# Building a small identity tile by DMA instead of by a GpSimd select, a first GpSimd maximum on zeros, and a buffer of its own for each of the last four results

## The chip, the cores and the metric

The kernel runs on one core of a Trainium2 chip. The metric is the device time of one execution in microseconds, as the median of several runs; lower is better. The engines are TensorE (PE, with its weight loads shown apart as PEld), VectorE (DVE), ScalarE (ACT), GpSimd (POOL) and the queue that issues the transfers (SP).

## The reference, cut to what matters

Linear attention with a learned feature map, then two MLPs without a residual. Shapes: batch 4, 8 heads, 576 positions, head dimension 64, 128 features, model width 512, hidden width 2048.

```python
def phi(x):
    proj = np.einsum('bhsd,df->bhsf', x, w_phi)
    proj = proj - np.max(np.abs(proj), axis=-1, keepdims=True)
    return np.concatenate([np.exp(proj), np.exp(-proj)], axis=-1)
q_p, k_p = phi(q), phi(k)
kv = np.einsum('bhsf,bhsd->bhfd', k_p, v)
z = np.sum(k_p, axis=2)
num = np.einsum('bhsf,bhfd->bhsd', q_p, kv)
den = np.einsum('bhsf,bhf->bhs', q_p, z)[..., None] + 1e-06
attn = num / den                        # then reshaped to 2304 tokens x 512
h = attn @ w_in;  x = (h * sigmoid(h)) @ w_out
h = np.maximum(x @ w_in2, 0.0);  out = (h * h) @ w_out2
```

The weights arrive as 64-bit floats (the kernel sees pairs of 32-bit words and converts them on DVE).

## The kernel before

Tokens are cut into 8 blocks of 288 columns. Each MLP handles a block in 16 chunks of 128 hidden units; the attention of the next blocks (keys of batch j and head pair p, queries of half batch b and head pair p) is mixed in between the chunks of the blocks before it. Most operands are split into a rounded high part and a low rest, so most products are three matmuls; keys and queries of the first blocks are multiplied whole.

No order of work is written out by hand. Every step is handed to a planner as an operation with an engine, a cost in ns, a key, and what it reads and writes (`op(key, engine, cost, emit, r=, w=, bufs=)`). The planner plays the engines through in its own time: on each idle engine the ready operation with the lowest key starts, if its buffers are free. A transfer costs it 640 ns on the queue, then its size at 240 bytes per ns behind all transfers before it, then 1500 ns (L70). ACT and DVE operations that belong to no unit get their key lowered by 202.77 (L86). The instructions are issued in the order that this gives, on five in-order queues; on the chip each waits for its own inputs. All transfers go through SP.

The start of the kernel, which the change touches:

- `phi_load` (L354) brings the feature weights into `wbl`, over zeros that `blank` set on DVE.
- `phi_zero` (L362) runs first on POOL, at a cost of 9000 in the plan: it builds the 65x65 identity `ident` with `make_identity` (a memset, masks.py:197, and an affine select, masks.py:199) and sets `wbl_hi` and `wbl_lo` to zero.
- `phi_hi` (L371, ACT) and `phi_lo` (L377, DVE) then split the feature weights into the high and low tiles that later blocks use.
- `queries_of` projects queries on PE (L792), copies them out on ACT (L798), takes the largest magnitude over all 128 partitions on POOL (`peak`, L805, tile `qm`), subtracts it on DVE (L811, tile `qp`) and exponentiates on ACT (L823, tile `qe`).
- `keys_of` projects keys (L602), takes their maximum (L607) and subtracts it (L613) on DVE, exponentiates (L690, tile `kp`), sets a column of ones in the value tile `v` on POOL (`ones`, L548) and multiplies features and values (L706, tile `pkv`). `v` has two buffers.
- The identity is read only by the transposes of `turn` (L732), from batch 2 on.

The end: the last chunk of a block copies its four accumulators to tiles `y` (L990 on ACT for d = 0 and 2, L992 on DVE for d = 1 and 3) and stores each (L995). These tiles have the tag `o`, with two buffers. The tag `xx`, also two buffers of the same shape, holds the attention's results `x`.

```python
LAT = {"PE": 450, "SP": 150}
DMA_ISSUE, DMA_LAT, DMA_RATE = 640, 1500, 240.0
...
op(T0 - 99, "POOL", 9000, phi_zero, w=["wbl0", "ident"])
op(P["phi"], "ACT", 1200, phi_hi, r=["wraw", "wbl0"], w=["phi_hi"])
op(P["phi"], "DVE", 1200, phi_lo, r=["wraw", "phi_hi"], w=["phi_lo"])
```

Of the kernel before, what the change touches and what calls it, by code (L numbers as in the profile page):

```python
# [9 lines left out]

F32 = mybir.dt.float32
F32R = mybir.dt.float32r
# [9 lines left out]
HB = S // 2  # L22
NB = NTOK // HB
# [5 lines left out]
D1 = D + 1  # L29
# [36 lines left out]
class Plan:  # L66
# [15 lines left out]
    def op(self, key, engine, cost, emit, r=(), w=(), bufs=(), unit=None, after=()):  # L82
        if unit and engine == "PE":
            key -= KEYS["pe"]
        if not unit and engine in ("ACT", "DVE"):
            key -= KEYS["el"]  # L86
        o = Op(len(self.ops), key, engine, cost, emit, unit)
        before = set(after)
        for x in r:
            before.update(self.written[x])  # L90
        for x in w:
            before.update(self.read.pop(x, ()))
            before.update(self.written.get(x, ()))
        for x in r:
            self.read.setdefault(x, []).append(o)
        for x in w:
            self.written[x] = [o]
        if unit and unit.token:
            bufs = [*bufs, unit.token]
        for b in bufs:  # L100
            if b not in self.started:
                self.started.add(b)
                b.first = o
                o.allocs.append(b)
                if b.pool in self.last:
                    self.last[b.pool][0] += 1
            else:
                before.add(b.first)
            b.users += 1
            o.frees.append(b)  # L110
        before.discard(o)
        o.waits = len(before)
        for x in before:
            x.after.append(o)
        self.ops.append(o)
        if unit:
            unit.ops.append(o)
        return o
# [131 lines left out]
def act(n, psum=False):  # L250
    return (51 if psum else 93) + 0.833 * n + 60


def dve(n, fast=False):
    return 70 + (0.52 if fast else 1.04) * n + 60
# [6 lines left out]
def dma(kb):  # L262
    return kb
# [14 lines left out]
def attention_then_two_mlps(ctx, tc, kT, qT, v, w_phi, w1, w2, out):  # L278
    nc = tc.nc
    P = KEYS  # L280
# [12 lines left out]
    sp = ctx.enter_context(tc.tile_pool(name="sp", bufs=2))  # L293
# [24 lines left out]
    op = plan.op  # L318
# [6 lines left out]
    def bank(name, unit, pool_="att"):  # L325
        if pool_ == "att" and unit.early == 2:
            pool_ = "eb"
        return Buf(pool_, lambda: psb.tile([128, 512], F32, tag="b", name=name), unit)

    def get(b):  # L330
        if b.tile is None:
            b.tile = b.make()
        return b.tile


    def hi_act(dst, src):
        nc.scalar.copy(out=dst, in_=src)  # L337

    def lo_on(engine, dst, src, hi):
        e = nc.vector if engine == "DVE" else nc.gpsimd  # L340
        e.tensor_tensor(out=dst, in0=src, in1=hi.bitcast(F32), op=ALU.subtract)  # L341
# [8 lines left out]
    ident = const.tile([D1, D1], F32, name="ident")  # L350
# [8 lines left out]
    def blank():  # L359
        nc.vector.memset(wbl, 0.0)  # L360

    def phi_zero():  # L362
        make_identity(nc, ident)
        nc.gpsimd.memset(wbl_hi.bitcast(F32), 0.0)
        nc.gpsimd.memset(wbl_lo.bitcast(F32), 0.0)

# [16 lines left out]
    T0 = -60.0  # L383
    op(T0 - 99, "DVE", 200, blank, w=["blank"])
    op(T0 - 99, "SP", dma(64), phi_load, r=["blank"], w=["wraw"])
    op(T0 - 99, "POOL", 9000, phi_zero, w=["wbl0", "ident"])
    op(P["phi"], "ACT", 1200, phi_hi, r=["wraw", "wbl0"], w=["phi_hi"])
    op(P["phi"], "DVE", 1200, phi_lo, r=["wraw", "phi_hi"], w=["phi_lo"])

# [523 lines left out]
    def chunk(L, i, c, key):  # L913
        n = f"{L}_{i}_{c}"
        b = L * NB + i
        C = ("c", L, i, c)
        w = wch[L, c]
        xb = xs[b]
        ps = bank("h" + n, None, "h")
        gb = Buf("g", lambda: [gp.tile([128, HB], dt, tag=t, name=t + n)  # L920
                               for t, dt in (("a", F32), ("gh", F32R), ("gl", F32R))], None)

        def gemm1():
            k = 0
            xh, xl = get(xb)
            ww = get(w)
            for cc in range(ND):
                f = slice(cc * 128, (cc + 1) * 128)
                for a, x in ((ww[:, 1, f], xh), (ww[:, 0, f], xl), (ww[:, 0, f], xh)):
                    nc.tensor.matmul(get(ps)[:, :HB], a, x[:, cc], start=k == 0, stop=k == 3 * ND - 1)  # L930
                    k += 1

        def f1():
            a = get(gb)[0]
            if L == 0:
                nc.scalar.activation(out=a, in_=get(ps)[:, :HB], func=AF.Tanh, scale=0.5)  # L936
            else:
                nc.scalar.activation(out=a, in_=get(ps)[:, :HB], func=AF.Relu)  # L938

        def f2():  # L940
            a = get(gb)[0]
            if L == 0:
                nc.vector.scalar_tensor_tensor(  # L943
                    out=a, in0=a, scalar=1.0, in1=get(ps)[:, :HB], op0=ALU.add, op1=ALU.mult
                )
            else:
                nc.vector.tensor_tensor(out=a, in0=get(ps)[:, :HB], in1=a, op=ALU.mult)  # L947

        def g_hi():
            hi_act(get(gb)[1], get(gb)[0])  # L950

        def g_lo():
            lo_on("DVE", get(gb)[2], get(gb)[0], get(gb)[1])

        W = [(("wf", L, c, 0), "hi"), (("wf", L, c, 0), "lo")]
        op(key, "PE", 3 * ND * MM, gemm1, r=W + [(t, b, p) for t in ("xh", "xl") for p in range(NP)],
           w=[(C, "h"), "order"], bufs=[ps, w, xb])
        op(key, "ACT", act(HB, True), f1, r=[(C, "h")], w=[(C, "a")], bufs=[ps, gb])
        op(key, "DVE", dve(HB), f2, r=[(C, "a")], w=[(C, "g")], bufs=[ps, gb])
        op(key, "ACT", act(HB), g_hi, r=[(C, "g")], w=[(C, "gh")], bufs=[gb])  # L960
        op(key, "DVE", dve(HB), g_lo, r=[(C, "g"), (C, "gh")], w=[(C, "gl")], bufs=[gb])
        W = [(("wf", L, c, 1), "hi"), (("wf", L, c, 1), "lo")]
        for d in range(ND):
            if c == 0:
                accs[L, i, d] = Buf(
                    "acc", lambda d=d: psb.tile([128, 512], F32, tag="b", name=f"o{L}_{i}_{d}"), None
                )
            acc = accs[L, i, d]

            def gemm2(d=d, acc=acc):  # L970
                _, gh, gl = get(gb)
                ww = get(w)
                f = slice(d * 128, (d + 1) * 128)
                for x, (a, g) in enumerate(((ww[:, 3, f], gh), (ww[:, 2, f], gl), (ww[:, 2, f], gh))):
                    nc.tensor.matmul(  # L975
                        get(acc)[:, :HB], a, g, start=c == 0 and x == 0, stop=c == NC - 1 and x == 2
                    )

            op(key + P["g2"], "PE", 3 * MM, gemm2, r=W + [(C, "gh"), (C, "gl")], w=[("acc", L, i, d)],
               bufs=[acc, gb, w])  # L980
        if c == NC - 1:
            for d in range(ND):
                acc = accs[L, i, d]
                y = Buf("o", lambda d=d: sp.tile([128, HB], F32, tag="o", name=f"y{L}_{i}_{d}"), None)
                e = "ACT" if d % 2 == 0 else "DVE"

                def evac(d=d, y=y, acc=acc):
                    m = 1.0 if L else 0.5
                    if d % 2 == 0:
                        nc.scalar.mul(out=get(y), in_=get(acc)[:, :HB], mul=m)  # L990
                    else:
                        nc.vector.tensor_scalar_mul(get(y), get(acc)[:, :HB], m)  # L992

                def store(d=d, y=y):
                    nc.sync.dma_start(out=(out if L else x2d)[:, d, i * HB:(i + 1) * HB], in_=get(y))  # L995

                op(key, e, act(HB) if e == "ACT" else dve(HB), evac, r=[("acc", L, i, d)], w=[("y", L, i, d)],
                   bufs=[acc, y])
                op(key, "SP", dma(144), store, r=[("y", L, i, d)], w=[("x2", L, i, d)], bufs=[y])
# [72 lines left out]
    for _, _, key, f, args in sorted(todo, key=lambda x: x[:2]):  # L1072
        if f == "key":
            args[0](key)
        elif f == "x2":
            x2_of(args[0], key)
        elif f == "chunk":
            chunk(*args, key)
        else:
            f(*args, key)  # L1080
# [42 lines left out]
```

## Time and profile before

| | |
|---|---|
| median of 3 runs | 1030.31 us (1029.76 to 1030.76) |
| the profiled execution's own time | 1030.11 us |
| its span, first to last instruction | 1028.3 us |
| PE busy | 1007.6 us, 98% of the span |
| DVE, ACT, POOL busy | 60%, 53%, 8% |
| mean granted TensorE clock | 0.990 of full speed |

The profile is one execution. The time of an execution holds 1.8 us around the span (1030.11 - 1028.3). Busy PE is a modelled figure, since matmuls are pipelined; what counts below is when an engine stands idle, what released it, and which clock PE was granted.

### The profile page before, as it was taken

What the parts mean: (1) busy time and instruction counts of PE and PEld (TensorE: products, weight loads), DVE (VectorE), ACT (ScalarE), POOL (GpSimd) and SP (SyncE); (2) the same over time, 40 slices, a digit from 0 to 9 for tenths busy, and PEclk for the clock granted to TensorE, in tenths of its full rate; (3) what the DMA queues carried; (4) which work ended last, traced back from release to release, by engine and by line L of the source; (5) the groups of instructions that cost most, each with busy time, mean ns of one, the idle gap of its engine ahead of it and who ended that gap; (6) DMA issues with size and microseconds to landing.
All of it is one profiled execution on the core that took longest, in us unless ns stands there. A gap on an engine that the chain in (4) does not pass through costs nothing.

```text
span 1028.3 us, 18934 instructions
## 1 busy us (share of the span) xinstructions
PE 1007.6 (98%) x7424; PEld 983.0 (96%) x7424; DVE 616.7 (60%) x1198; ACT 547.5 (53%) x1338; POOL 80.0 (8%) x56
## 2 busy tenths in 40 slices
PE   7879999999999999999999999999999999999998
PEld 6759899999999999999999999999999999999997
DVE  4789997876657766788987684333333333333222
ACT  4757876778776787775654563232322323232222
POOL 2340003210022100201100000000000000000000
PEclk8989999999999999999999999999999999999999
DMA  8336511232003223456565951010101010100000
GB/s 282 111 126 224 186 66 36 60 84 74 24 14 92 65 57 94 139 144 201 164 180 177 311 186 47 1 47 1 47 1 47 1 47 1 47 7 18 12 13 24
DMA packets 48761, 88.95 MB, mean 87 GB/s; under 512 B 12192, under 2 KB 24608, under 8 KB 46624
## 3 DMA queue, kind: packets, MB, share of 16 engines
q1 hardware_dynamic: 48672, 87.74, 27.4%
q8 instruction: 58, 0.95, 0.4%
q14 instruction: 31, 0.25, 0.1%
HBM read 69.75 MB, written 17.90 MB: 85 GB/s over the span
## 4 chain that ended last, share of the span: by engine, by line
PE 90%; DVE 6%; issue 2%; DMA 1%; POOL 0%; ACT 0%; POOLq 0%; ACTq 0%; DVEq 0%
PE o L975 38%; PE h L930 38%; PE pn L857 4%; PE pkv L706 3%; PE pkv L663 3%; PE pk L602 2%; DVE w L341 1%; DVE wc L443 1%; PE pq L794 1%; DVE wc L447 1%; DMA rr<-qn 1%; PE pq L795 1%; DVE x L895 1%; DVE wc L439 0%; DVE mx L607 0%
## 5 line engine op out<-in xcount | busy, mean ns | idle before, releaser
L975 PE MATMUL o<-gh,w 128*128 128x288 f32 x2048 | 457.5, 296 | 0.0
L930 PE MATMUL h<-x,w 128*128 128x288 f32 x3072 | 449.7, 295 | 1.6 <-DVE w L341 1.6
L930 PEld LDWEIGHTS h<-x,w 128*128 128x128 f32 x3072 | 421.3, 188 | 3.0 <-issue 1.7
L975 PEld LDWEIGHTS o<-gh,w 128*128 128x128 f32 x2048 | 344.6, 188 | 2.5 <-issue 1.1
L975 PE MATMUL o<-gl,w 128*128 128x288 f32 x1024 | 301.9, 295 | 0.1
L975 PEld LDWEIGHTS o<-gl,w 128*128 128x128 f32 x1024 | 192.4, 188 | 0.6 <-DVE gl L341 0.5
L947 DVE TENSOR_TENSOR a<-h,a 128x288 f32<-128x288 f32 x128 | 58.6, 458 | 214.2 <-ACT a L938 214.2
L938 ACT ACTIVATE a<-h 128x288 f32<-128x288 f32 x128 | 52.7, 412 | 225.4 <-PE h L930 225.4
L341 DVE TENSOR_TENSOR gl<-a,gh 128x288 fp32r<-128x288 f32 x256 | 120.8, 472 | 69.1 <-ACT gh L337 51.0
L337 ACT CAST gh<-a 128x288 fp32r<-128x288 f32 x256 | 111.4, 436 | 75.6 <-DVE a L947 57.0
L805 POOL PARTITION_ALL_REDUCE qm<-qp x32 | 77.5, 2437 | 302.8 <-ACT qp L798 260.2
L936 ACT ACTIVATE a<-h 128x288 f32<-128x288 f32 x128 | 52.9, 414 | 61.3 <-PE h L930 60.2
L943 DVE SCALAR_TENSOR_TENSOR a<-a,h 128x288 f32<-128x288 f32 x128 | 57.6, 450 | 40.8 <-ACT a L936 40.0
L706 PEld LDWEIGHTS pkv<-v,kp 128*128 128x128 f32 (+1 forms) x320 | 41.4, 210 | 7.9 <-POOL v L548 6.8
L706 PE MATMUL pkv<-v,kp 128*128 128x128 f32 (+1 forms) x320 | 43.2, 297 | 5.9 <-POOL v L548 5.9
L823 ACT ACTIVATE qe<-qp 128x576 f32<-128x576 f32 x64 | 41.7, 681 | 7.6 <-DVE qp L811 7.5
L635 ACT ACTIVATE ke<-pk,mx 128x128 f32<-128x128 f32 (+1 forms) x160 | 44.6, 376 | 0.0
L857 PE MATMUL pn<-qh,kv 128*65 128x288 f32 x192 | 41.4, 294 | 0.0
L607 DVE TENSOR_REDUCE mx<-pk 128x4 f32<-128x512 f32 (+1 forms) x48 | 28.2, 595 | 21.0 <-PE pk L602 20.7
L341 DVE TENSOR_TENSOR qo<-qe,qh 128x576 fp32r<-128x576 f32 x48 | 35.8, 750 | 2.1 <-ACT qh L337 0.9
L860 ACT COPY qn<-pn 65x288 f32<-65x288 f32 x64 | 24.9, 394 | 20.7 <-PE pn L857 20.2
L811 DVE TENSOR_TENSOR qp<-qp,qm 128x576 f32<-128x576 f32 x32 | 26.5, 829 | 10.6 <-POOL qm L805 10.6
(87 smaller groups left out, 974.9 us busy)
## 6 DMA issues: line engine op xcount, KB each, us to landing
wbits<-w SPq DMA_DIRECT2D x16, 1024.0 KB, 5.8
wr<-w SPq DMA_DIRECT2D x32, 512.0 KB, 4.9
w2d<-wc SPq DMA_DIRECT2D x32, 256.0 KB, 2.7
w2f<-w2d SPq DMA_DIRECT2D x32, 256.0 KB, 4.1
qr<-qT SPq DMA_DIRECT2D x56, 144.0 KB, 3.0
v<-v SPq DMA_DIRECT2D x16, 325.0 KB, 3.3
kr<-kT SPq DMA_DIRECT2D x16, 288.0 KB, 3.5
qb<-rd SPq DMA_DIRECT2D x32, 144.0 KB, 3.1
```

The source lines that it names most:

```text
L337: nc.scalar.copy(out=dst, in_=src)
L341: e.tensor_tensor(out=dst, in0=src, in1=hi.bitcast(F32), op=ALU.subtract)
L635: nc.scalar.activation(out=get(e)[:nt, a, s], in_=get(ps)[:nt, x * F:(x + 1) * F], func=AF.Exp, scale=1.0 - 2.0 * s, bias=get(mx)[:nt, s, ...
L706: nc.tensor.matmul(get(ps)[:, o:o + 128], get(kps[2 * g + s])[:nt, 2 * i + a], get(vt)[:nt, c:c + 128], start=t == 0 and a == 0 and s == 0 ...
L805: nc.gpsimd.partition_all_reduce(get(mx), get(pr).rearrange("p a t -> p (a t)"), 128, bass.bass_isa.ReduceOp.absmax)
L857: nc.tensor.matmul(get(ps)[:D1, :HB], w, get(e)[:, t], start=x == 0, stop=x == len(ops) - 1)
L930: nc.tensor.matmul(get(ps)[:, :HB], a, x[:, cc], start=k == 0, stop=k == 3 * ND - 1)
L936: nc.scalar.activation(out=a, in_=get(ps)[:, :HB], func=AF.Tanh, scale=0.5)
L938: nc.scalar.activation(out=a, in_=get(ps)[:, :HB], func=AF.Relu)
L943: nc.vector.scalar_tensor_tensor(out=a, in0=a, scalar=1.0, in1=get(ps)[:, :HB], op0=ALU.add, op1=ALU.mult)
L947: nc.vector.tensor_tensor(out=a, in0=get(ps)[:, :HB], in1=a, op=ALU.mult)
L975: nc.tensor.matmul(get(acc)[:, :HB], a, g, start=c == 0 and x == 0, stop=c == NC - 1 and x == 2)
```

## The change

The affine select is gone. POOL now sets `ident` to zero and takes a maximum over part of it (64 partitions, 8 columns, all zeros) with the operation that the queries use. The zeroing of `wbl_hi` and `wbl_lo` becomes an operation of its own with a later key. The identity comes about through a DRAM tile `idd`: the zeros are stored there, DVE sets the first row of `ident` to ones, that row is stored onto the diagonal of `idd` (65 single elements), and the whole is loaded back: three transfers on SP, each after the one before. Two of the last block's four results use the tag `xx`.

```diff
+    def fetch():
+        nc.gpsimd.memset(ident, 0.0)
+        nc.gpsimd.partition_all_reduce(ident[:64, :8], ident[:64, :8], 64, bass.bass_isa.ReduceOp.absmax)
+    idd = tc.dram_tile([D1, D1], F32, name="idd")
+    def id_one():
+        nc.vector.memset(ident[:1], 1.0)
+    def id_zeros_out():
+        nc.sync.dma_start(out=idd, in_=ident)
+    def id_ones_out():
+        flat = idd.rearrange("a b -> (a b)")
+        nc.sync.dma_start(out=flat[0:D1 * D1:D1 + 1].rearrange("(o n) -> o n", o=1), in_=ident[:1])
+    def id_load():
+        nc.sync.dma_start(out=ident, in_=idd)
     def phi_zero():
-        make_identity(nc, ident)
         nc.gpsimd.memset(wbl_hi.bitcast(F32), 0.0)
         nc.gpsimd.memset(wbl_lo.bitcast(F32), 0.0)
...
-    op(T0 - 99, "POOL", 9000, phi_zero, w=["wbl0", "ident"])
+    op(T0 - 99, "POOL", 9000, fetch, w=["id0"])
+    op(P["phi"] - 10, "POOL", 600, phi_zero, w=["wbl0"])
+    op(P["phi"], "SP", dma(17), id_zeros_out, r=["id0"], w=["id1"])
+    op(P["phi"], "DVE", 150, id_one, r=["id1"], w=["id0"])
+    op(P["phi"], "SP", dma(1), id_ones_out, r=["id0", "id1"], w=["id2"])
+    op(P["phi"], "SP", dma(17), id_load, r=["id2"], w=["id0", "ident"])
...
-                y = Buf("o", lambda d=d: sp.tile([128, HB], F32, tag="o", name=f"y{L}_{i}_{d}"), None)
+                tag = "xx" if L and i == NB - 1 and d >= 2 else "o"
+                y = Buf(tag, lambda d=d, tag=tag: sp.tile([128, HB], F32, tag=tag, name=f"y{L}_{i}_{d}"), None)
```

## Rows read from the trace of the kernel before

**Rows 1.** The page, part 1: busy time, share of the span, instructions.

```profile
PE 1007.6 (98%) x7424; PEld 983.0 (96%) x7424; DVE 616.7 (60%) x1198; ACT 547.5 (53%) x1338; POOL 80.0 (8%) x56
```

**Rows 2.** Busy time by stretch; the last three columns: granted clock, DMA share, GB/s.

```profile
15.00:20.00 5.00, 1.72 (x7) 1.04 (x7) 0.36 (x1) 0.80 (x2) 2.55 (x4) 0.87 1.04 329
20.00:25.00 5.00, 5.00 (x24) 5.00 (x25) 5.00 (x8) 3.30 (x7) 2.16 (x2) 0.50 1.02 321
...
45.00:50.00 5.00, 4.61 (x26) 4.62 (x27) 4.69 (x6) 4.65 (x9) 1.97 (x4) 0.66 0.00 0
```

**Rows 3.** The chain that ended last, 0 to 20 us: start, length, what.

```profile
0.95 7.90 issue
8.86 0.23 POOL ident masks.py:199
9.09 0.26 POOL wbl_hi L364
...
9.84 6.12 issue
...
15.97 1.48 issue
17.45 2.15 POOL qm L805
```

**Rows 4.** Lines masks.py:199 and, up to 60 us, L805: durations in ns (min/median/max).

```profile
masks.py:199 POOLq MODIFY_POOL_CONFIG  x2: 11/11/11, 0.9 to 0.9; - x2
...
L805 POOL PARTITION_ALL_REDUCE qm<-qp x5: 2154/2604/3439, 17.5 to 48.4; - x5
L805 POOLq MODIFY_POOL_CONFIG  x2: 1/1/1, 9.8 to 9.8; - x2
```

**Rows 5.** Timeline of PE: start, length, group, idle before it and its releaser.

```profile
14.24 2.20 PE L792 MATMUL pq<-qr,wbl 64*128 64x288 f32 x8
19.73 7.65 PE L706 MATMUL pkv<-v,kp 128*128 128x128 f32 x40 [3.28 <-POOL v L548]
...
28.28 4.82 PE L706 MATMUL pkv<-v,kp 128*128 128x128 f32 x40
```

**Rows 6.** Timeline of DVE (two rows), then of ACT (four rows).

```profile
12.46 0.27 DVE L381 TENSOR_TENSOR wst_lo<-wbl,wst_hi 64x128 fp32r<-64x128 f32 x1
...
19.64 1.96 DVE L811 TENSOR_TENSOR qp<-qp,qm 128x576 f32<-128x576 f32 x1 [6.19 <-POOL qm L805]
...
10.31 0.88 ACT L798 COPY qp<-pq 128x288 f32<-128x288 f32 x2
11.09 0.30 ACT L374 CAST wst_hi<-wbl 64x128 fp32r<-64x128 f32 x1
...
15.03 0.88 ACT L798 COPY qp<-pq 128x288 f32<-128x288 f32 x2 [1.16 <-PE pq L792]
21.70 1.26 ACT L823 ACTIVATE qe<-qp 128x576 f32<-128x576 f32 x2 [5.78 <-DVE qp L811]
```

**Rows 7.** SP's waits to 60 us; transfers issued 9 to 17 us; `rr`; L732.

```profile
SPq L551 <- PE pkv L706: 18.9, 2, 13.6
...
wbits<-w SPq DMA_DIRECT2D x2, 1024.0 KB, 13.4
...
DMA to landing us min/median/max: 1.9/1.9/3.2
...
L732 PE MATMUL pkt<-ident,kvT x32: 220/224/226, 247.3 to 429.1; 65*128 65x65 f32 x32
```

**Rows 8.** DVE's busy time in one stretch; then clock, DMA share, GB/s.

```profile
58.20:107.00 48.80, 48.03 (x84) 0.93 0.55 190
```

**Rows 9.** Timeline of the end: PE, DVE, SP.

```profile
1023.07 0.29 PE L975 MATMUL o<-gh,w 128*128 128x288 f32 x1
...
1022.61 0.46 DVE L992 TENSOR_SCALAR y<-o 128x288 f32<-128x288 f32 x1 [2.04 <-PE o L975]
1025.04 0.46 DVE L992 TENSOR_SCALAR y<-o 128x288 f32<-128x288 f32 x1 [1.97 <-DMA out<-y]
...
1022.65 3.20 SPq L995 DMA_DIRECT2D out<-y  x4
```

More of the change, by code (lines that the diff above doesn't have):

```diff
@@ L8 @@
 from concourse._compat import with_exitstack
-from concourse.masks import make_identity
 F32 = mybir.dt.float32
```

## The prediction, made before the changed kernel ran

> **What bounds the kernel now.** I read the page first. PE is busy for 1007.6 us of a span of 1028.3 [rows 1], so all idle of PE together is 20.7 us, and the question for any edit is which of that idle it touches. The busy time by stretch shows where it is: between 15 and 20 us PE works for 1.72 of 5 us, and the granted clock then falls, to 0.87 in that stretch and 0.50 in the next [rows 2], which is the lower level, 1.2 GHz, for all of it. The change touches the start and the end.
>
> For the start I followed the chain that ended last. Its first 20 us stand on POOL and are mostly not work: 7.90 us of "issue" ahead of the affine select, 6.12 and 1.48 us ahead of the first maximum `qm`, against 0.23 us for the select and 2.15 us for the maximum [rows 3]. The instruction view says what opens each gap: a pair of MODIFY_POOL_CONFIG at 0.9 us under the select's line, and a pair at 9.8 us under the maximum's [rows 4]. So POOL is set up twice, for two kinds of operation, at 7.90 us and 6.12 + 1.48 = 7.60 us. There is no third pair up to 60 us, though memsets of `v` stand between the five maxima counted there: a memset does not cost a new set-up, nor does a further maximum.
>
> What waits for it: the first maximum's input is two copies on ACT that end at 10.31 + 0.88 = 11.19 us, yet it starts at 17.45 us and ends at 19.60 us. Behind it on POOL stand the memsets of `v`; they release PE's `pkv` at 19.73 us, after 3.28 us idle [rows 5]. DVE's subtraction L811 waits for the maximum too, 6.19 us, to 19.64 us; ACT's exponential L823 5.78 us, to 21.70 us [rows 6].
>
> Downstream, DVE is busy for 48.03 of the 48.80 us from 58.2 to 107 [rows 8]: in that stretch its work sets the pace, and it begins as early as the stage ahead lets it. So whatever is won at the start must pass a stretch bound by DVE; it passes whole if DVE's work is the same and begins earlier.
>
> At the end, the third and fourth results wait for a buffer: the fourth's copy stands idle for 1.97 us until a store has landed and starts at 1025.04 us, though PE's last matmul ended at 1023.07 + 0.29 = 1023.36 [rows 9].
>
> **The change, part by part.**
>
> *One set-up instead of two.* The select's pair goes; the maximum's pair moves to 0.95 us. By the two measured set-ups the maximum on zeros starts between 0.95 + 7.60 = 8.55 and 0.95 + 7.90 = 8.85 us. Its own time is not in the trace (64x8 against 128x576): at least nothing, at most the 2.15 us of the fastest full one. So it ends between 8.6 and 11.0 us, ahead of the first real input at 11.19 us. That input now decides, and it does not depend on POOL. The first real maximum runs from 11.2 us. It took 2.15 us with DVE idle beside it, up to 3.44 us among other work [rows 4]: end 13.4 to 14.7 us. I take 13.4, since DVE's two-input instructions that stood here (`phi_lo`, L381, four like the row [rows 6]) move behind it.
>
> The Trainium skill, SBUF — State Buffer, section "Who interferes with whom", speaks against an early maximum: GpSimd and VectorE share one port pair as an exclusive lock. By it I would take 14.7; the trace agrees that a maximum can last 3.44 us. The sum is the same by both, because PE and ACT, below, are not ready for the result before 15.9.
>
> *What that gives PE.* Its work before `pkv` ends at 14.24 + 2.20 = 16.44 us [rows 5], and by then the memsets of `v` are done (13.6 to 15.0; with the two memsets of `phi_zero`, 0.26 us by the row, put in ahead, 14.1 to 15.5). Idle saved: 19.73 - 16.44 = 3.29 us. Then the clock: `pkv` at the low clock took 7.65 us, the next one, of the same 40 matmuls, 4.82 [rows 5]. If PE does not stand idle, I expect the clock to stay at 2.4 GHz: 2.83 us more, 6.1 together. The other fall shown, 0.66 from 45 to 50 us [rows 2], lies in another wait and stays. Bounds: 3.3 (the clock falls all the same) to 6.1.
>
> *What it gives DVE and ACT.* L811 moves from 19.64 to 13.4 us: 6.2 us. L823 can start when ACT has ended its copies at 15.03 + 0.88 = 15.91 us instead of 21.70: 5.8 us. The three engines thus move by 5.8 to 6.2 us; I take 6.0 for what reaches the DVE stretch and, through it, the end.
>
> *phi_zero, phi_hi and phi_lo later.* ACT has four copies like the 0.30 us row (start to start they fill 11.09 to 12.1 us) and DVE four subtractions; they keep a very low key and run when POOL has zeroed the tiles. Covered, they cost nothing: POOL gets the first maximum's input at 11.19 and the second's only at 15.91 [rows 6], so the two memsets fit in between, and ACT's copies before 15.91. Uncovered, they cost ACT 1.0 us behind 15.91. I take 0.
>
> *The three transfers and one memset for the identity.* The first reader of `ident` is at 247.3 us [rows 7], so they are late for nobody; their price could only be what queues behind them. On SP: loads of `v` wait until PE frees a buffer at 27.46 us, 13.6 us [rows 7]; the last weight load ahead of that left at 13.3 to 13.8 us, so there is room. A transfer of 2 KB lands in 1.9 us when the queues are calm. Two waits of that kind, 4 us, delay what stands behind on SP, and that (the small `rr` spreads and the next weights) is needed later. I take 0; the upper bound is the rival below. The Trainium skill, DMA: Bandwidth & Descriptors, section "Anatomy of one DMA — SWDGE (gpsimd) path", puts about 2 us of fixed cost on a transfer, most of it the receipt of the last write; it is told for another issuer than SP. By it the chain of three takes at least 6 us, as an estimate; the rows that bear on it are the landings of `rr`, 1.9 us each, and the sum stays the same by both, since nobody reads the identity before 247.3 us.
>
> *Four buffers at the end.* The fourth copy starts behind PE's last matmul, 1023.4 instead of 1025.04: 1.6 us. SP issued four stores in 3.20 us with two waits among them; four in a row fit into the 1.6 us that is left if each takes under 0.4 us. Bounds: 1.0 (issue in a queue, four stores landing together) to 1.64. I take 1.6.
>
> **Sum.** 6.0 + 1.6 = 7.6 us off the profiled execution's 1030.11 gives 1022.5; that execution lies 0.20 below the median 1030.31, so I forecast 1022.6 for the median.
>
> One thing is left without a row: the plan is made anew, and the operations with new places can turn the order of others in the first 160 us. I allow 2 us either way for it.
>
> **The rivals.**
>
> 1. *Half the start.* PE is idle no longer, but the clock falls all the same, or ACT gets the `phi_hi` copies in the wrong place: 3.3 + 1.6 = 4.9 off, 1025.4. For it: the clock fell within a stretch that began with PE at work [rows 2]. Against: 3.28 us of idle lie ahead of the fall and would be gone.
> 2. *The start is hidden.* Something that does not move takes over before 58 us, most likely the weights: a load issued between 9 and 17 us took 13.4 us to land [rows 7], with the DMA engines full (share 1.04 and 1.02 [rows 2]). Then only the tail is left: 1028.7. Against: the last of these land at about 13.3 + 13.4 = 26.7 us and ACT takes up the first only behind L823 and what follows.
> 3. *The set-up is not gone.* POOL sets up the maximum again at its first real use, or the 7.90 us belong to any first operation and the second price remains: the start is as before, the tail gains, 1028.7. Against: two pairs under two lines, none elsewhere.
> 4. *Slower: VectorE held by the identity.* `id_one` on DVE waits for the store of zeros. If that store leaves behind the last weight load (13.3 us), it lands behind its backlog, at about 26.7 us. DVE takes its queue in order: if `id_one` stands ahead of L811, then L811 starts at 26.7, not 19.64, 7.1 us later than before; with the tail 1030.3 + 7.1 - 1.6 = 1035.8. It decides the sign once DVE is held beyond 19.64 + 1.6 = 21.2 us. Against: the plan moves 240 bytes per ns and counts the early loads (7.1 MB by the sizes in the code) as landed only after some 30 us, while the chip moved 321 to 329 GB/s [rows 2]; so the plan should place `id_one` later than the chip could run it, behind L811.
> 5. *More.* Maxima and DVE fall apart in time, L811 at 1.96 us gets shorter, and another wait closes: 1020.
>
> **How the numbers follow.** What a measurement of this kernel can tell from no change is about 0.2%, 2.1 us: faster is under 1028.2, slower over 1032.4. Forecast 0.62 (1021 to 1024.6 with the plan's 2 us), rival 1 0.15, rival 2 0.07, rival 3 0.04, rival 4 0.07, rival 5 0.05. Faster: forecast, 1, 5 and a quarter of 2 and 3, 0.85; same: the rest of 2 and 3, 0.08; slower: 0.07. The range runs from rival 5's inner side, 1019.5, to behind rival 1, 1027.0; it leaves out 2, 3, 4: 0.18.
>
> **What would show it.** Right: no MODIFY_POOL_CONFIG under L805; the first `qm` on a query at 11 to 12 us; `pkv` from about 16.5 us in under 5 us, granted clock near 1 from 15 to 25 us; the DVE stretch begins about 6 us earlier and is as full; the four copies at the end within 1.3 us. Wrong: a second pair at the first query (3), DVE idle ahead of `id_one` (4), `pkv` at 7 us again (1), a new idle of PE between 25 and 110 us (2 or the order).

## The result and the profile after

The changed kernel takes 1036.08 us (median of 4 runs, 1034.78 to 1036.56) against 1030.24 us for the kernel before, a ratio of 1.0055 with a 95% interval of 1.0037 to 1.0072: slower by 5.8 us where 7.6 us less was forecast. The profiled execution took 1034.78 us, with a span of 1033.0 us.

PE's start came out as forecast. Three views of the changed kernel: the instructions of the line of the maximum on zeros (durations in ns), the timeline of POOL and that of PE (start, length, group, idle before it and its releaser).

```profile
L364 POOLq MODIFY_POOL_CONFIG  x2: 8/8/8, 0.9 to 0.9; - x2
L364 POOL PARTITION_ALL_REDUCE ident<-ident x1: 362/362/362, 1.0 to 1.0; - x1
```

```profile
1.01 0.36 POOL L364 PARTITION_ALL_REDUCE ident<-ident  x1
1.23 0.41 POOL L383 MEMSET wbl_hi<- 128x256 f32 x1
1.48 0.41 POOL L384 MEMSET wbl_lo<- 128x256 f32 x1
10.41 2.16 POOL L829 PARTITION_ALL_REDUCE qm<-qp  x1 [8.53 <-ACT qp L822]
```

```profile
14.93 1.23 PE L816 MATMUL pq<-qr,wbl 64*128 64x288 f32 x4
16.09 9.78 PE L730 MATMUL pkv<-v,kp 128*128 128x128 f32 x80
...
63.39 4.10 PE L881 MATMUL pn<-qe,kv 128*65 128x288 f32 x8 [7.65 <-ACT qe L847]
```

There is one pair of MODIFY_POOL_CONFIG, where [rows 4] showed two. The first maximum on a query starts at 10.41 us, released by its input from ACT; in [rows 3] it started at 17.45. PE runs into `pkv` without a pause at 16.09 us, where [rows 5] showed 3.28 us of idle and a start at 19.73. The two products take 9.78 us for 80 matmuls, where the first 40 alone took 7.65.

The waits of PE over the whole execution (us in total, times, longest) show where the time went instead:

```profile
PE pn L881 <- ACT qh L336: 7.8, 1, 7.8
PE pn L881 <- ACT qe L847: 7.7, 1, 7.7
PE pq L818 <- DVE ql L340: 3.5, 2, 2.3
```

The first of them is new: one wait of 7.8 us. It lies at 501.8 to 509.6 us, far from the edit. The busy time by stretch, in the columns of [rows 2], of the changed kernel and then of the kernel before:

```profile
0.00:160.00 160.00, 146.80 (x921) 124.89 (x922) 141.93 (x218) 113.89 (x271) 28.55 (x27) 0.96 0.48 160
160.00:500.00 340.00, 339.81 (x2602) 336.71 (x2600) 244.57 (x488) 241.12 (x625) 38.24 (x25) 1.00 0.30 87
500.00:515.00 15.00, 5.92 (x25) 5.14 (x26) 10.94 (x21) 7.14 (x16) 2.31 (x2) 0.66 0.55 162
```

```profile
0.00:160.00 160.00, 144.38 (x878) 123.16 (x879) 134.70 (x208) 109.82 (x257) 29.52 (x26) 0.95 0.48 160
160.00:500.00 340.00, 339.88 (x2602) 336.72 (x2601) 252.64 (x503) 251.16 (x651) 47.55 (x30) 1.00 0.30 87
500.00:515.00 15.00, 15.00 (x115) 15.00 (x115) 13.71 (x30) 9.40 (x22) 2.51 (x2) 1.00 0.55 183
```

Read the counts of matmuls in the second column. By 160 us the changed kernel has done 921 - 878 = 43 more; at the steady 115 matmuls in 15 us, 7.7 per us, that is a lead of about 5.6 us. From 160 to 500 us the two go at one pace. Then, from 500 to 515 us, it does 25 where the other does 115: 90 matmuls, about 11.7 us, with PE idle for 9.1 of the 15 us and a mean clock of 0.66. From there on the pace is the same again.

The chain that ended last, in that stretch of the changed kernel (start, length, what), shows what PE waits for:

```profile
497.04 2.48 PE o L999 x19
499.52 3.11 DMA qb<-rd
502.63 0.02 issue
502.65 1.30 DVE x L919
503.96 0.01 issue
503.97 0.46 DVE x L919
...
506.87 0.77 DVE qp L835
...
507.71 0.74 ACT qe L847 x2
...
508.87 0.66 ACT qh L336
...
510.37 2.90 PE pn L881 x11
```

DVE's queue comes to a multiplication (L919) that needs the broadcast load `qb`, which lands at 502.63 us. Behind it in the queue lie more multiplications, the subtraction (L835) and, through ACT, the queries that PE needs next. DVE itself stands idle for this load for only 0.62 us. The maximum that L835 subtracts ran on POOL from 502.36 to 504.50 us, so DVE's queue holds these queries up by 2.4 us (506.87 - 504.50); the other 5.4 of the 7.8 us are their own way from PE's projection over ACT, POOL, DVE and ACT back to PE. This way costs time here because PE has nothing else to do: it has run out of MLP work ahead of block 6. The last of the four pieces of that block's input is done by DVE at 514.53 us, and the block's first matmuls follow at 514.94. Three rows of the changed kernel (the POOL maximum, DVE's last piece, PE's first matmuls of block 6), then DVE's last piece of block 6 in the kernel before, 25 us earlier:

```profile
502.36 2.14 POOL L829 PARTITION_ALL_REDUCE qm<-qp  x1 [20.79 <-DMA rr<-qn]
514.07 0.46 DVE L340 TENSOR_TENSOR x<-x,x 128x288 fp32r<-128x288 f32 x1 [0.68 <-ACT x L336]
514.94 1.23 PE L954 MATMUL h<-x,w 128*128 128x288 f32 x8
```

```profile
488.76 0.45 DVE L341 TENSOR_TENSOR x<-x,x 128x288 fp32r<-128x288 f32 x1
```

The end did as forecast: the four copies run from 1028.32 to 1029.97 us, the fourth 0.04 us behind PE's last matmul, and no copy waits for a store. The rows are DVE's and SP's timeline of the changed kernel, against [rows 9]:

```profile
1028.71 0.46 DVE L1018 TENSOR_SCALAR y<-o 128x288 f32<-128x288 f32 x1 [2.04 <-PE o L999]
1029.51 0.46 DVE L1018 TENSOR_SCALAR y<-o 128x288 f32<-128x288 f32 x1 [0.34 <-PE o L999]
...
1028.76 1.79 SPq L1021 DMA_DIRECT2D out<-y  x4
```

The lead of 5.6 us, the stall of 11.7 and a tail shorter by about 1.4 (from PE's last end to the span's end 3.5 instead of 4.9 us) make 4.7 us, the difference of the two spans. The medians lie 5.8 us apart, because the profiled execution is the fastest of the four.

### The profile page after: what moved, and what is told of

Same layout as the page of the kernel before. It is cut to its first block, busy times and chain, and to the rows that moved or that the text cites. A ratio compares the mean times of both kernels' runs of the same rounds, so it can differ in the third digit from the quotient of the medians.

```text
span 1033.0 us, 18934 instructions
## 1 busy us (share of the span) xinstructions
PE 1007.0 (97%) x7424; PEld 981.0 (95%) x7424; DVE 621.4 (60%) x1199; ACT 547.8 (53%) x1338; POOL 75.3 (7%) x56
## 4 chain that ended last, share of the span: by engine, by line
PE 95%; DVE 3%; ACT 1%; issue 0%; DMA 0%; POOL 0%; ACTq 0%; DVEq 0%
PE h L954 39%; PE o L999 39%; PE pn L881 5%; PE pk L626 3%; PE pkv L687 3%; PE pkv L730 3%; PE pq L818 1%; PE pq L819 1%; DVE wc L471 1%; DVE wc L467 0%; PE pq L816 0%; DVE x L919 0%; DVE qp L835 0%; PE warm L423 0%; DVE w L340 0%
## 5 line engine op out<-in xcount | busy, mean ns | idle before, releaser
L829 POOL PARTITION_ALL_REDUCE qm<-qp x32 | 71.7, 2263 | 305.5 <-ACT qp L822 284.7
L730 PEld LDWEIGHTS pkv<-v,kp 128*128 128x128 f32 (+1 forms) x320 | 37.0, 191 | 3.5 <-POOL v L572 1.9
L730 PE MATMUL pkv<-v,kp 128*128 128x128 f32 (+1 forms) x320 | 38.9, 278 | 0.9 <-POOL v L572 0.8
L881 PEld LDWEIGHTS pn<-qh,kv 128*65 128x65 f32 x192 | 26.4, 139 | 8.1 <-ACT qh L336 8.0
```

Source lines behind the costliest of these rows:

```text
L730: nc.tensor.matmul(get(ps)[:, o:o + 128], get(kps[2 * g + s])[:nt, 2 * i + a], get(vt)[:nt, c:c + 128], start=t == 0 and a == 0 and s == 0 ...
L829: nc.gpsimd.partition_all_reduce(get(mx), get(pr).rearrange("p a t -> p (a t)"), 128, bass.bass_isa.ReduceOp.absmax)
L881: nc.tensor.matmul(get(ps)[:D1, :HB], w, get(e)[:, t], start=x == 0, stop=x == len(ops) - 1)
```

## The experiments

The theory after the result (A): the work that the change removes is won, but the plan, made anew, gives another order, and that order starves PE ahead of block 6. The rivals: the early maximum or the identity's transfers cost time by themselves (B), the start's gain is hidden further on in any order (C), or the loss is spread over the whole order (D).

Why the order differs can be read off the planner. The zeroing of `wbl_hi` and `wbl_lo`, now an operation of its own with a planned 600 ns, is planned right behind `fetch`. On POOL the instructions at the start then stand as they would anyway, but in the planner's time the first maximum moves from 9.49 to 9.60 us, and `phi_hi` on ACT falls behind one more exponential. PE's order differs from its 12th operation on. In the planner's time the last piece of block 6's input then comes at 508.8 us instead of 475.1. Which of the many exchanges in between brings that about is not shown.

**e1_joined: the whole change, in the old order.** The zeroing goes back into the first POOL operation; no instruction is added or left out. Apart from the operations for the identity, the order is that of the kernel before on every engine but for two neighbours on ACT, which change places at 48 us of the plan.

```diff
-    op(T0 - 99, "POOL", 9000, fetch, w=["id0"])
-    op(P["phi"] - 10, "POOL", 600, phi_zero, w=["wbl0"])
+    op(T0 - 99, "POOL", 9000, lambda: (fetch(), phi_zero()), w=["id0", "wbl0"])
```

> The whole change, but the zeroing of wbl_hi and wbl_lo stays inside the first POOL operation, as before, so that PE and POOL get the order of before instruction for instruction. Theory A (the changed order loses what the start wins): the start's 6 to 8 us and the tail's 1.6 us are both there, 1021 to 1024 us, no idle of PE over 1 us near 510 us. Rival B (the early maximum or the three transfers cost by themselves, whatever the order): within 2 us of the changed kernel, 1034 to 1038. Rival C (the start's gain is hidden further on even in the old order): 1027 to 1030.

Measured: 1023.32 us (before 1030.1; ratio 0.9934, 0.9919 to 0.9948). A holds, B and C fall: with the same instructions the old order is 12.8 us faster than the new one (12.5 by the two ratios to the kernel before, which ran beside each). Its busy time by stretch has no hole at 500 us:

```profile
0.00:160.00 160.00, 147.61 (x915) 126.49 (x916) 138.96 (x217) 113.75 (x266) 30.64 (x26) 0.96 0.48 160
160.00:500.00 340.00, 339.71 (x2602) 336.68 (x2601) 252.74 (x506) 248.83 (x648) 47.22 (x29) 1.00 0.32 89
500.00:515.00 15.00, 15.00 (x116) 15.00 (x115) 13.66 (x31) 11.11 (x25) 2.14 (x1) 1.00 0.54 167
```

**e2_old_setup: the new order, with the select again.** The planner's operations stay; the first builds the identity with the select, and the transfers are not issued.

```diff
     def fetch():
-        nc.gpsimd.memset(ident, 0.0)
-        nc.gpsimd.partition_all_reduce(ident[:64, :8], ident[:64, :8], 64, bass.bass_isa.ReduceOp.absmax)
+        make_identity(nc, ident)
...
     def id_one():
+        pass
+    id_zeros_out = id_ones_out = id_load = id_one
```

> The changed kernel's plan and order, but the first POOL operation builds the identity with the select as before (two set-ups), and the three transfers and the memset of the first row are not issued. Theory A: the start's gain is taken back under the new order, so it is slower than the changed kernel by 4 to 8 us, 1040 to 1044. Rival B: with the early maximum and the transfers gone the loss is gone as well, 1029 to 1031. Rival C (the start is hidden in any order): as the changed kernel, 1035 to 1037.

Measured: 1039.11 us (1036.7 to 1042.5; ratio 1.0079, 1.0062 to 1.0097), 3.0 us slower than the changed kernel by the medians. That is under the 4 to 8 expected of A, in a scatter of 5.8 us, so it does not part A from C well (C had expected 1035 to 1037; e1 did that). But it is no recovery (B). Its PE stands idle for the same 7.8 us, without the early maximum and without the transfers. The waits of PE in this kernel:

```profile
PE pn L871 <- ACT qh L337: 7.8, 1, 7.8
PE pn L871 <- ACT qe L837: 7.7, 1, 7.7
PE pkv L720 <- POOL v L562: 5.0, 2, 4.2
```

**e3_tail_only: the four buffers alone, on the kernel before.**

```diff
-                y = Buf("o", lambda d=d: sp.tile([128, HB], F32, tag="o", name=f"y{L}_{i}_{d}"), None)
+                tag = "xx" if L and i == NB - 1 and d >= 2 else "o"
+                y = Buf(tag, lambda d=d, tag=tag: sp.tile([128, HB], F32, tag=tag, name=f"y{L}_{i}_{d}"), None)
```

> The kernel before with the four buffers at the end alone; the order is that of before throughout. All theories: 1.3 to 1.7 us faster, 1028.5 to 1029.0; if four stores in flight hinder each other, 0 to 1 us faster.

Measured: 1028.61 us (ratio 0.9983, 0.9974 to 0.9993): 1.5 us less, as expected.

**e4_plan_cost: the order alone.** One planned cost of the kernel before is changed; the instructions are the same.

```diff
-    op(T0 - 99, "POOL", 9000, phi_zero, w=["wbl0", "ident"])
+    op(T0 - 99, "POOL", 10000, phi_zero, w=["wbl0", "ident"])
```

> The kernel before with one number changed, the planned cost of its first POOL operation, 10000 instead of 9000: every instruction is the same, only their order differs, as the plan makes it anew. Theory A: the order alone moves the time by several us, most likely to the slower side, 1034 to 1046, with a new idle of PE in the attention part. Rival B or C: within 2 us of 1030.

Measured: 1049.86 us (ratio 1.0191, 1.0173 to 1.0208), 19.8 us slower and beyond the range expected. One number that no instruction carries is worth more than either half of the change. The waits of PE in this kernel; the 5.6 us in the first row end at 517 us:

```profile
PE pq L794 <- DVE ql L341: 9.0, 3, 5.6
PE pn L857 <- ACT qe L823: 7.8, 1, 7.8
PE pkv L706 <- POOL v L548: 6.5, 2, 3.7
PE pn L857 <- DVE qo L341: 3.2, 1, 3.2
```

**e5_late_key: the stall alone.** On the changed kernel, block 6's queries get a key 0.5 later. The planned order stays that of the changed kernel up to about 360 us.

```diff
-                want(t + 32 - P["qe"] + P["qs"] * p, queries_of, 2 * j + 2, p)
+                want(t + 32 - P["qe"] + 0.5 * (j == 2) + P["qs"] * p, queries_of, 2 * j + 2, p)
```

> The changed kernel with one key moved: the queries of block 6 get a key that is 0.5 later, which leaves the planned order as it is up to about 360 us and alters it after that. Theory A (the loss against the old order sits in the stall of PE ahead of block 6, 7.79 + 1.19 us of idle between 501 and 515 us and the low clock there): 1022 to 1026 us, with no idle of PE over 1 us from 400 us on. Rival D (the loss is spread over the new order, or made at the start): 1032 to 1036.

Measured: 1023.3 us (ratio 0.9939, 0.9923 to 0.9956). The start of every MLP chunk up to 340 us lies within 0.5 us of the changed kernel's, PE no longer waits for `qh`, and 12.8 us are gone (11.9 by the ratios to the kernel before, which took 1029.56 us beside this run). D falls: the loss lay behind 360 us, and the changed kernel's only idle of PE there is that stall. In the busy time by stretch of this kernel it is filled:

```profile
500.00:515.00 15.00, 15.00 (x115) 15.00 (x115) 14.16 (x29) 8.05 (x20) 4.26 (x2) 1.00 0.60 194
```

**e6_late_transfers: the joined version, the identity later.** The planner's four operations issue nothing; the instructions follow at fixed places of the order, at 168 to 183 us of the plan.

```diff
+    nothing = lambda: None
-    op(P["phi"], "SP", dma(17), id_zeros_out, r=["id0"], w=["id1"])
+    op(P["phi"], "SP", dma(17), nothing, r=["id0"], w=["id1"])
...
-        for o in plan.run():
+        for n, o in enumerate(plan.run()):
+            for f in {700: [id_zeros_out], 740: [id_one, id_ones_out], 780: [id_load]}.get(n, ()):
+                f()
```

> The joined version (order of before, one set-up, four buffers), with the three transfers and the memset of the first row issued at about 165 to 185 us of the plan instead of 15 to 37 us; the plan is the same. Theory A (they cost nothing where they are): as the joined version, 1022.3 to 1024.3. Rival B (SP or DVE is held by them at the start): 1 to 3 us faster, 1020.5 to 1022.

Measured: 1023.91 us (ratio 0.9946, 0.9931 to 0.9961), not told apart from e1's 0.9934. Where they stand, the transfers cost nothing that can be measured.

**e7_no_first_max: the joined version without the maximum on zeros.**

```diff
         nc.gpsimd.memset(ident, 0.0)
-        nc.gpsimd.partition_all_reduce(ident[:64, :8], ident[:64, :8], 64, bass.bass_isa.ReduceOp.absmax)
```

> The joined version without the maximum on zeros. If the set-up for a maximum takes the 7.6 us that it took behind the select, and the maximum on zeros hides it: the first maximum on a query starts at about 17 to 19 us instead of 11, and the time is 1026 to 1030. If a maximum is what GpSimd is set up for anyway, and the select was the odd one: no pause, as the joined version, 1022.3 to 1024.3.

Measured: 1023.48 us (ratio 0.9942, 0.9928 to 0.9957), as e1. The maximum on zeros is worth nothing: what counted was to leave out the select. The line of the maxima up to 60 us, and POOL's timeline, in this kernel:

```profile
L827 POOL PARTITION_ALL_REDUCE qm<-qp x7: 2140/2157/3453, 11.1 to 59.6; - x7
L827 POOLq MODIFY_POOL_CONFIG  x2: 8/8/8, 1.4 to 1.4; - x2
```

```profile
11.05 2.14 POOL L827 PARTITION_ALL_REDUCE qm<-qp  x1 [9.68 <-ACT qp L820]
```

Four versions thus take 1023.3 to 1023.9 us: e1_joined and its variants e6 and e7, and e5_late_key, which keeps the planned start of the changed kernel.

The planner bears this out by itself. It keeps the end of its own time (`length`), and its order can be made without the chip. In microseconds:

| | planned end | planned, against before | measured, against before |
|---|---|---|---|
| before | 1014.7 | | |
| changed kernel | 1026.4 | +11.8 | +5.8 |
| e1_joined | 1012.8 | -1.9 | -6.8 |
| e4_plan_cost | 1031.5 | +16.8 | +19.8 |
| e5_late_key | 1013.4 | -1.2 | -6.3 |

The plan gives the first POOL operation 9 to 10 us in every version, so it cannot see what the start wins, but it prices the orders: the changed kernel against e1 is 13.7 us there and 12.8 on the chip. It also shows the place: in the changed kernel's plan PE stands idle for 8.9 us from 497.1 us on, in that of e4 for 5.9 and 4.9 us from 497.5 and 503.9 us on, and in the plans of before, e1 and e5 it has no idle over 0.3 us from 150 us on.

## Why the prediction was wrong, step by step

*One set-up instead of two, and the input decides: right.* One pair is left, and the first maximum waits for ACT alone. That the maximum on zeros would start at 8.55 to 8.85 us was wrong (1.01 us), and without effect, as the input at 10.4 us decides anyway. Nor was that maximum needed: in e7, without it, the pair stands at 1.4 us and the first maximum on a query starts at 11.05, when its input is there.

*PE at 16.44 us and the clock at 2.4 GHz: right.* 16.09 us, clock 1.00 up to 25 us, and 80 matmuls in 9.78 us. *DVE from 13.4 us: right* (L835 at 13.14 us), although `phi_lo` did not move behind the maximum as assumed (it ran from 12.13 us) and the maximum took 2.16 us all the same.

*6.0 us reach the end: right in kind, mis-sized.* In the old order (e1) the span shrinks by 6.3 us; less the tail of 1.4 this leaves 4.9 (by the medians 6.8 less 1.5, 5.3). The loss is seen at the third and fourth `pkv`: 80 matmuls took 12.69 us, before 11.40, behind nearly the same idle (2.64 us, before 2.62). PE's lead over the kernel before falls there from 6.55 us (38.84 against 45.39) by 1.3. The low clock (0.50, the lower level, 1.2 GHz) lasted longer: 0.50 in every microsecond from 39 to 45 us, where before it was 0.50 from 46 to 49 us and 0.81 in the next. The prediction had put this fall down as unchanged; why it lasted longer is open. PE's timeline and the busy time of these matmuls, in e1 and then in the kernel before:

```profile
38.84 12.69 PE L729 MATMUL pkv<-v,kp 128*128 128x128 f32 x80 [2.64 <-POOL v L571]
38.84:51.53 12.69, 12.69 (x81) 12.20 (x82) 10.38 (x14) 4.62 (x9) 2.62 (x1) 0.76 0.29 102
```

```profile
45.39 11.40 PE L706 MATMUL pkv<-v,kp 128*128 128x128 f32 x80 [2.62 <-POOL v L548]
45.39:56.79 11.40, 11.40 (x81) 10.92 (x82) 10.37 (x14) 4.63 (x9) 2.60 (x1) 0.85 0.17 50
```

*The zeroing and the feature weights at no cost: right on the chip, and the trigger of the loss in the plan.* They were expected behind the first maximum; the planner put them ahead of it, since at 9.0 us of its time no maximum was ready.

*The transfers at no cost: right* (e6). Rival 4 names nearly the time that was measured (1035.8), but by chance: its mechanism did not occur, `id_one` ran on DVE at 33.89 us, long behind L835. *The four buffers 1.6: right* (e3, 1.5).

*The step that failed* is the one "left without a row": "I allow 2 us either way" for the order, and "in the first 160 us". The order was worth 12.8 us (1036.08 against 1023.32), and it lost them at 501 to 515 us, 340 us behind the stretch that was looked at. With 12.8 put in for the 2, and the other terms as measured, the sum is 1030.2 - 4.9 - 1.5 + 12.8 = 1036.6, measured 1036.1; as both the 4.9 and the 12.8 are taken from e1, this closes nearly by itself and is no check. A row for this term was at hand: the planner's own end moves by 11.8 us with the edit. The error in the reasoning was to price the edit by its instructions. Here a planned cost is part of the program: it decides the order of all that follows, and stretches where PE is busy without a gap before, as from 160 to 1000 us, are no evidence that another order fills them as well. (Two slips in the prediction's sums change nothing: 1022.5 + 0.20 is 1022.7, not 1022.6, and 11.2 + 3.44 is 14.6, not 14.7.)

## What to carry to other kernels

Where a planner makes the order, an edit has two prices, that of its instructions and that of the new order, and the second can be the larger and lie far behind the edit. Measure the first with the order held (as in e1), and the second with the instructions held (as in e4), before judging the edit. Ahead of both, read the planner's own end and the idle of the bounding engine in its time, before and after the edit: here they gave the place of the loss, and its size within 1 us (within 3 us in e4). When a gain at the start does not reach the end, count the work done by the bounding engine up to several points of time: the stretch where the lead is lost names the wait.

## What the runs showed of the hardware that was not expected

A set-up of POOL (its pair of MODIFY_POOL_CONFIG) did not pause it every time. Ahead of the select it took 7.90 us, and ahead of a maximum that follows a select 7.60 us [rows 3]; but where a maximum is the first such operation, it ran 0.1 us behind its MODIFY_POOL_CONFIG, in 0.36 us, and the memset behind it at 1.23 us. The Trainium skill, GPSIMD Engine Reference, section "2.1 Instruction dispatch", says that the first call to a freshly loaded kernel pays about 6 us; the 6.12 us ahead of the first maximum behind a select [rows 3] come near that, the 7.90 us ahead of the select are more, and the first maximum of the changed kernel shows no such pause. Whether its code was there from the start, or is loaded behind records that end early, stays open: in e7 the first real maximum comes 9.7 us behind its pair, which would hide either.

A fall of PE's clock behind nearly the same idle did not cost the same: 2.62 and 2.64 us of idle were followed by 11.40 and 12.69 us for the same 80 matmuls, at a mean granted clock of 0.85 and 0.76.
